# Two transposers for one tile: TensorE takes the lower halves of the probabilities in the first two batches

## The chip, the cores and the metric

The kernel runs on one core of one Trainium2 chip. The metric is the device time of one execution in microseconds (us). Beside it there is a trace of one profiled execution; its own time and its span are in the table further down.

## The reference

An attention layer, then two feed-forward layers, all in fp32: 4 batches, 8 heads, 576 positions, head size 64.

```python
scores = scale * np.matmul(q, k.transpose(0, 1, 3, 2))
h = np.maximum(x @ w1 + b1, 0.0)               # x[i, j]: a function of the positions i and j
scores = scores + (h @ w2).transpose(2, 0, 1)[None]
attn = np.exp(scores - np.max(scores, axis=-1, keepdims=True))
attn = attn / (np.sum(attn, axis=-1, keepdims=True) + 1e-09)
x = np.matmul(attn, v)                         # 2304 tokens x 512
h = x @ w_in;  solu = h * softmax(h)           # 1024 wide
x = (layer_norm(solu) * g_ln) @ w_out
out = (sigmoid(x @ w_gate) * (x @ w_val)) @ w_out2     # 1536 wide
```

The weights of the feed-forward layers come as 8-byte floats. Every fp32 factor of a product is split into a high and a low fp16 part, and three fp16 products (high by high, high by low, low by high) are summed.

## The kernel before, in words

**Attention is cut into 72 ticks** (the list `ticks`, filled by `block`). A tick is 128 queries of two heads against all 576 keys of a batch. A block has 16 ticks for 256 queries of two batches, or 4 ticks ("M") for the last 64 queries of two batches together; batches 0 and 1 are ticks 0 to 35, batches 2 and 3 are ticks 36 to 71. The first element of a tick, `bp`, is 0 or 1 for the two pairs of batches.

**One tick's work** passes through five functions. `a_qk` puts the scores into PSUM (TensorE, L530). `a_soft` adds the bias and takes the maximum (VectorE, L550), scales the maximum (ScalarE, L555) and takes the exponential (ScalarE, L557) into the tile `p` of 2 x 576 fp32. `a_split` makes the fp16 tile `p16` of 2 x 1152 columns: the high part is a cast, on VectorE in every fourth tick (L566) and on ScalarE in the others (L568); the low part is `p` minus the high part on GpSimd, 2 x 512 columns first (L569), then the 2 x 64 columns of the last keys (L570), which fill the second half of a block that the high part's last 64 columns begin. So `p16` has 18 blocks of 128 columns, 9 for each head: 5 with the high part (the fifth is half high, half low) and 4 with the low part of 512 keys. One DMA, issued on SyncE's queue (L572), transposes all 18 into the tile `pt`. `a_pv` multiplies `pt` with V (TensorE, L590; 28 products a tick, 56 of half the width in an M tick) into `xps`. `a_x` and `a_xt` divide by the sums, and transpose the result on TensorE (L636).

**The order.** The loop at the end of the attention emits, in step t: `a_qk(t)`, `a_soft(t)`, `a_split(t-1)`, `a_x(t-5)`, some items of side work, preparation of Q, K and V (`prep_q` L280 to L283, `prep_k` L241 to L244, `prep_v` L254 and L255; their transposes go through PSUM), `a_pv(t-4)`, `a_xt(t-5)`. A planner orders the instructions of every engine from these, by priority and by its own estimate of the times. From the step in which the side work has passed `open_moe` on, TensorE alone is bound to the written order (`manual_schedule`).

**The side work** is first the bias of the later query blocks (masks on VectorE L393, products on TensorE L444, sums on VectorE L460 and L464, stores to memory) and the decoding and splitting of the weights of the first feed-forward layer (loads L660; ScalarE L172, L683, L667 and L668; VectorE L173, L174 and L177; GpSimd L181 and L669). After `open_moe` it is the first feed-forward layer of finished token tiles (TensorE `hps` L732, `ltp` L777, `x2ps` L791), three items a step. `hps` and `x2ps` are sums that are built over several items and hold their PSUM buffer meanwhile.

**Buffers.** `p16` has 2 buffers at first and 3 after `open_moe`, `pt` 3 and then 4. PSUM is cut into `ps_s` (2 buffers of two banks, scores), `ps_v` (1, `xps`) and `ps_m` (3 buffers of one bank), through which go the transposes of Q, K, the attention's result and the feed-forward layer (`qtp`, `ktp`, `xtp`, `ltp`), half of the bias products (`bp`), `hps` and `x2ps`.

After the attention come the weights of the second feed-forward layer and its products (L1149 to L1339); these lines are the same before and after.

Of the kernel before, what the change touches and what calls it, by code (L numbers as in the profile page):

```python
# [9 lines left out]
F16 = mybir.dt.float16  # L10
BF16 = mybir.dt.bfloat16
I32 = mybir.dt.int32
ACTF = mybir.ActivationFunctionType
ALU = mybir.AluOpType
# [78 lines left out]
def attn_moe_kernel(  # L93
# [7 lines left out]
    act, dve, pool, pe, sp = nc.scalar, nc.vector, nc.gpsimd, nc.tensor, nc.sync  # L101
    AX = mybir.AxisListType.X

    def enter(stack, name, bufs=1, side="left", space=None):
        kw = {} if space is None else {"space": space}
        if space is None:
            kw["reuse_waits"] = "tile"
            kw["side"] = side
        return stack.enter_context(tc.tile_pool(name=name, bufs=bufs, **kw))
# [5 lines left out]
    const = enter(ctx, "const")  # L115
# [7 lines left out]
    ps_m = enter(pss, "ps_m", 3, space=PSUM)  # L123
    ps_v = enter(pss, "ps_v", 1, space=PSUM)

    ones_sb = const.tile([128, 128], F32, name="ones_sb")
    id_sb = const.tile([128, 128], F32, name="id_sb")
    sc = const.tile([128, 32], F32, name="sc")
    gs = const.tile([128, 8], F32, name="gs")
    nhalf = const.tile([128, 1], F32, name="nhalf")  # L130
# [33 lines left out]
    def flat(a):  # L164
        return a.rearrange("b h s d -> (b h s d)").rearrange("(p f) -> p f", p=128)
# [27 lines left out]
    def ring(nm, shape, dt, tag=None):  # L193
        r = rings[nm]
        n = turn.get(nm, 0) % len(r)
        turn[nm] = n + 1
        return r[n].tile(shape, dt, name=nm, tag=tag or nm)


    raws, KT, VT, QT = {}, {}, {}, {}  # L200
# [4 lines left out]
    def load_raw(src, b, hp, nm):  # L205
        waiting.append((src, b, hp, nm))
        load_waiting()
# [52 lines left out]
    def load_q(key):  # L260
        bp, qd, hp, b = key
        if qd == "M":
            t = qraw_p.tile([128, 2, 2, D], F32, name="qraw", tag="qraw")
            for par in range(2):
                sp.dma_start(out=t[64 * par:64 * par + 64, 0],
                             in_=q[2 * bp + par, 2 * hp:2 * hp + 2, 512:576, :].rearrange("h p d -> p h d"))
        else:
            t = qraw_p.tile([128, 2, 2, D], F32, name="qraw", tag="qraw")
            for h in range(2):
                sp.dma_start(out=t[:, :, h, :], in_=q[2 * bp + b, 2 * hp + h, 256 * qd:256 * qd + 256, :]  # L270
                             .rearrange("(p r) d -> p r d", r=2))
        raws[key] = t
# [215 lines left out]
    def store0(t, hp):  # L488
        sp.dma_start(out=bias_d[t, :, 2 * hp:2 * hp + 2, :], in_=gb0[t][:, 2 * hp:2 * hp + 2])
# [7 lines left out]
    def load_bias(tk):  # L497
        bp, qd, hp, r, _, bset = tk
        key = (bp, qd, hp, r, bset)
        if key in brt:  # L500
            return
        if (bp, qd) == (0, 0):
            brt[key] = [gb0[r][:, 2 * hp + hh, :] for hh in range(2)]
            return
        n = 8 + 2 * (nbr[0] % 4)
        nbr[0] += 1
        t = gk[0][:, n:n + 2, 0:S]
        if qd == "M":
            for par in range(2):
                sp.dma_start(out=t[64 * par:64 * par + 64], in_=bias_d[4, 0:64, 2 * hp:2 * hp + 2, :])  # L510
        else:
            sp.dma_start(out=t, in_=bias_d[2 * qd + r, :, 2 * hp:2 * hp + 2, :])
        brt[key] = [t[:, hh, :] for hh in range(2)]

    st1, st2, st3, xps, sums, xns = {}, {}, {}, {}, {}, {}
# [44 lines left out]

    def a_split(i):
        pp = st2.pop(i)
        p16 = ring("p16", [128, 2, 1152], F16)
        hi = p16[:, :, 0:576]
        if i % 4 in HI_DVE:
            dve.tensor_copy(hi, pp)  # L566
        else:
            act.activation(out=hi, in_=pp, func=ACTF.Copy)  # L568
        pool.tensor_tensor(out=p16[:, :, 640:1152], in0=pp[:, :, 0:512], in1=hi[:, :, 0:512], op=ALU.subtract)  # L569
        pool.tensor_tensor(out=p16[:, :, 576:640], in0=pp[:, :, 512:576], in1=hi[:, :, 512:576], op=ALU.subtract)  # L570
        pt = ring("pt", [128, 2, 9, 128], F16)
        sp.dma_start_transpose(out=pt.rearrange("p r c q -> p (r c) q"), in_=p16.rearrange("p r c -> p (r c)"))  # L572
        st3[i] = pt

    def pv_seq(vt, hh, lhs):
        seq = []
        for c in range(5):
            seq.append((lhs(c), vt[:, hh, c]))
            seq.append((lhs(c), vt[:, hh, 5 + c]))
        for c in range(4):  # L580
            seq.append((lhs(5 + c), vt[:, hh, c]))
        return seq

    def a_pv(i):
        bp, qd, hp, r, b, bset = ticks[i]
        pt = st3.pop(i)

        def run(seq, o):
            for n, (a, b_) in enumerate(seq):
                pe.matmul(o, a, b_, start=(n == 0), stop=(n == len(seq) - 1))  # L590

        if qd == "M":
            x = ps_v.tile([128, 512], F32, name="xps", tag="v")
            for hh in range(2):
                for par in range(2):
                    po = slice(64 * par, 64 * par + 64)
                    run(pv_seq(VT[2 * bp + par, hp], hh, lambda c: pt[:, hh, c, po]),
                        x[po, 64 * hh:64 * hh + 64])
            xps[bp, qd, hp, bset] = x
        else:  # L600
            key = (bp, qd, hp, bset)
            if key not in xps:
                xps[key] = ps_v.tile([128, 512], F32, name="xps", tag="v")
            x = xps[key]
            for hh in range(2):
                o = 256 * bset.index(b) + 128 * r + 64 * hh
                run(pv_seq(VT[2 * bp + b, hp], hh, lambda c: pt[:, hh, c, :]), x[:, o:o + 64])

    def a_x(i):
        bp, qd, hp, r, b, bset = ticks[i]  # L610
# [193 lines left out]
    ticks, tiles, ready = [], [], []  # L804
# [102 lines left out]
    def stats(src, w):  # L907
        a = nst[0]
        n = src.shape[1] // w
        for i in range(n):  # L910
            t = raw_p.tile([128, w], F32, name="sraw", tag="sraw")
            sp.dma_start(out=t, in_=src[:, w * i:w * i + w])
            j = sj_p.tile([128, w], BF16, name="sj", tag="sj")
            act.activation(out=j, in_=t, func=ACTF.Square, accum_out=stat[:, nst[0]:nst[0] + 1])
            nst[0] += 1
        return (a, nst[0])
# [13 lines left out]
    bs["mid"] = load_mid(bs["sign"])  # L930
    ck = stats(flat(k), SW)
    sp.dma_start(out=id_sb, in_=ident)
    load_q((0, 0, 0, 0))
    load_raw(k, 0, 0, "k")
    with tc.high_priority(1000):
# [70 lines left out]
    def side_step(t):  # L1006
        if nxt[0] is None or (t is not None and nxt[0][0] > t):
            return False
        nxt[0][1]()
        nxt[0] = next(it, None)  # L1010
        return True

    def until(key):
        while key not in done:
            assert side_step(None)
# [3 lines left out]
    for t in range(nticks + LAG_PV + LAG_X + 1):  # L1019
        if not own and "open" in done:  # L1020
            own.append(in_order.enter_context(tc.manual_schedule(engines={mybir.EngineType.PE})))
        with tc.high_priority(PRIO):
            for f in at.get(t, []):
                f()
        for u in range(t, t + 3):
            if u < nticks:
                for tt in {0: (), 1: (2, 3), "M": (4,)}[ticks[u][1]]:
                    until(("bias", tt))
                load_bias(ticks[u])
        with tc.high_priority(PRIO):  # L1030
            if t < nticks:
                a_qk(t)
                a_soft(t)
            if 0 <= t - 1 < nticks:
                a_split(t - 1)
            if 0 <= t - LAG_PV - LAG_X < nticks:
                a_x(t - LAG_PV - LAG_X)
        if t % 2 == ST0 % 2 and 0 <= t - ST0 < 16:
            store0((t - ST0) // 2 % 2, (t - ST0) // 4)
        for n in range(NB if "s" in glob else NB0):  # L1040
            side_step(t)
            if n == 0:
                with tc.high_priority(PRIO):
                    for f in late.get(t, []):
                        f()
        with tc.high_priority(PRIO):
            if 0 <= t - LAG_PV < nticks:
                a_pv(t - LAG_PV)
            if 0 <= t - LAG_PV - LAG_X < nticks:
                a_xt(t - LAG_PV - LAG_X)  # L1050
# [322 lines left out]
    for g in range(2, 5):  # L1373
        n = sizes[g]
# [75 lines left out]
```

## Time and profile before

| what | us |
|---|---|
| three runs | 1086.48, 1092.41, 1091.01 |
| their median | 1091.01 |
| the profiled execution's own time | 1090.94 |
| its span, first to last instruction | 1089.2 |
| busy in the span: TensorE, VectorE, ScalarE, GpSimd | 914.1, 777.0, 619.7, 404.3 |
| mean granted TensorE clock | 0.893 of full speed |
| bytes moved by DMA | 146.58 MB |

In the rows below "A <- B" reads "A waited for B"; SPq is SyncE's queue, which only issues DMAs, and its durations are the time that an issue took. The DMA share of a stretch is the busy share of 16 DMA engines; packets are counted where they start, so it can pass 1.

### The profile page before, as it was taken

The page shows a single profiled execution, that of the slowest core. Times are in us where ns is not written, and L with a number is a line of the kernel's source. Part 1 is how long each engine was busy: PE and PEld are TensorE (multiplying, and loading weights), DVE is VectorE, ACT ScalarE, POOL GpSimd, SP SyncE. Part 2 cuts the span into 40 slices and gives each one's busy share as a digit, 9 for nine tenths or more (in the row PEclk, how much of TensorE's full clock was granted, in tenths as well). Part 3 has the DMA queues.
Part 4 walks back from the last instruction along what each step waited for, and adds up shares of the span by engine and source line. Part 5 has one row for each costly group of instructions (what it writes and reads, how often), then busy time and mean ns, then how long its engine had stood idle before and what let it go on. Part 6 is the DMA issues. An engine that isn't in the chain of part 4 may idle for free.

```text
span 1089.2 us, 24462 instructions
## 1 busy us (share of the span) xinstructions
PE 914.1 (84%) x9806; PEld 655.5 (60%) x9806; DVE 777.0 (71%) x1605; ACT 619.7 (57%) x1283; POOL 404.3 (37%) x370
## 2 busy tenths in 40 slices
PE   3645674669688879989999788897999999999998
PEld 3634554546466658667776466444477866865873
DVE  6875998895666676666765999989973871881760
ACT  4786776765676788877883676753442331331331
POOL 2356355653555565545561365749000000000000
PEclk9655566778898999989999898999999999999999
DMA  7999999489879899998975535511001010001001
GB/s 226 289 293 254 215 218 244 99 182 230 165 162 191 197 194 180 195 189 196 189 113 169 163 111 174 187 56 39 30 11 58 1 49 30 1 1 39 2 1 39
DMA packets 261442, 146.58 MB, mean 135 GB/s; under 512 B 217680, under 2 KB 231504, under 8 KB 261328
## 3 DMA queue, kind: packets, MB, share of 16 engines
q1 hardware_dynamic: 259264, 143.18, 55.2%
q0 software_dynamic: 1536, 1.58, 0.6%
q8 instruction: 77, 1.26, 0.5%
q14 instruction: 37, 0.30, 0.1%
q10 hardware_dynamic: 528, 0.26, 0.1%
HBM read 82.46 MB, written 20.05 MB: 94 GB/s over the span
## 4 chain that ended last, share of the span: by engine, by line
PE 30%; DVE 13%; DMA 4%; ACT 2%; issue 2%; SPq 0%; ACTq 0%; DVEq 0%
PE prod L1262 15%; PE ops L1330 10%; DVE fs L1186 4%; DVE w2f L177 2%; DVE w2f L174 2%; DMA wraw<-in_moe_w_val_dram 2%; PE x2ps L791 2%; PE s_ps L1300 1%; DVE w2s L1186 1%; DMA wraw<-in_moe_w_gate_dram 1%; DVE gv L1168 1%; PE hps L732 1%; DMA wraw<-in_moe_w_out_dram 1%; DVE fr L1306 1%; PE xps L590 1%
## 5 line engine op out<-in xcount | busy, mean ns | idle before, releaser
L569 POOL TENSOR_TENSOR p<-p,p 128x1024 f16<-128x1024 f32 x72 | 155.7, 2162 | 155.0 <-ACT p L568 116.6
L1186 DVE TENSOR_TENSOR fr<-prod,fr 128x512 f32<-128x512 f32 x126 | 85.1, 687 | 94.0 <-PE prod L1262 92.3
L1330 PE MATMUL ops<-w2f,gv 128*128 128x512 f16 x648 | 143.4, 379 | 2.7 <-POOL w2f L669 1.5
L557 ACT ACTIVATE p<-p,m,sc 128x576 f32<-128x576 f32 x144 | 123.9, 861 | 2.8
L791 PE MATMUL x2ps<-lt,w1f 128*128 128x128 f16 x1728 | 111.9, 226 | 12.4 <-DVE lt L780 11.7
L550 DVE CUSTOM_DVE_ANT_0 p<-s_ps,gk 128x576 f32<-128x576 f32 x144 | 104.2, 751 | 20.3 <-PE s_ps L530 16.4
L791 PEld LDWEIGHTS <-w1f 128*128 128x128 f16 x1728 | 105.7, 102 | 21.1 <-issue 17.0
L1300 PE MATMUL s_ps<-xb,w2f 128*128 128x512 f16 (+1 forms) x576 | 101.5, 333 | 15.0 <-DVE fr L1306 10.7
L590 PE MATMUL xps<-gk,pt 128*128 128x64 f16 (+1 forms) x2240 | 89.2, 204 | 23.0 <-DMA pt<-p 23.0
L1330 PEld LDWEIGHTS <-gv 128*128 128x128 f16 x648 | 63.4, 98 | 74.4 <-issue 1.5
L590 PEld LDWEIGHTS <-pt 128*128 128x128 f16 (+1 forms) x2240 | 83.3, 108 | 34.8 <-DMA pt<-p 25.5
L530 PE MATMUL s_ps<-gk,qt 64*128 64x288 f16 (+1 forms) x960 | 92.1, 321 | 13.2 <-DVE m L550 6.9
L444 PEld LDWEIGHTS <-mask 128*128 128x128 f16 (+1 forms) x1312 | 64.5, 122 | 51.1 <-issue 18.0
L1300 PEld LDWEIGHTS <-w2f 128*128 128x128 f16 x576 | 57.3, 100 | 58.7 <-issue 22.7
L1262 PEld LDWEIGHTS <-w2f 128*128 128x128 f16 x864 | 84.5, 98 | 11.8 <-issue 1.1
L1167 ACT ACTIVATE gv<-fr 128x512 f16<-128x512 f32 (+1 forms) x60 | 34.9, 585 | 83.7 <-DVE fr L1320 70.5
L732 PE MATMUL hps<-w1f,xt 128*128 128x512 f16 x312 | 76.7, 396 | 0.6 <-DVE qt L283 0.6
L555 ACT ACTIVATE m<-m,sc 128x1 f32<-128x1 f32 x144 | 40.6, 286 | 54.1 <-DVE m L550 53.9
L444 PE MATMUL bp<-rhs,mask 128*128 128x64 f16 (+1 forms) x960 | 51.3, 224 | 22.5 <-DVE gb L464 13.9
L530 PEld LDWEIGHTS <-qt 64*128 64x128 f16 (+1 forms) x960 | 47.3, 106 | 36.8 <-issue 16.8
L1262 PEld LDWEIGHTS <-w2s 128*128 128x128 f16 x648 | 63.4, 98 | 7.3
L732 PEld LDWEIGHTS <-xt 128*128 128x128 f16 x384 | 37.1, 102 | 49.8 <-issue 15.5
(194 smaller groups left out, 1795.2 us busy)
## 6 DMA issues: line engine op xcount, KB each, us to landing
gk<-bias_d SPq DMA_DIRECT2D x24, 576.0 KB
wraw<-in_moe_w_out_dram SPq DMA_DIRECT2D x20, 512.0 KB
wraw<-in_moe_w_gate_dram SPq DMA_DIRECT2D x12, 512.0 KB
wraw<-in_moe_w_val_dram SPq DMA_DIRECT2D x12, 512.0 KB
sraw<-in_q_dram SPq DMA_DIRECT2D x12, 384.0 KB
sraw<-in_k_dram SPq DMA_DIRECT2D x12, 384.0 KB
sraw<-in_v_dram SPq DMA_DIRECT2D x12, 384.0 KB
bias_d<-gk SPq DMA_DIRECT2D x8, 576.0 KB
```

The lines of the kernel that those rows point to most:

```text
L444: pe.matmul(big[0:np_, jj // 8, o:o + 64], lhsT, rhs[i].rearrange("p c h g -> p (c h g)"), start=(i == 0), stop=(i == 1),)
L530: pe.matmul(ss[hh][p0:p1, n, 0:288], qt[rows, nr * ql + r, p0:p1], kt[rows, o:o + 288], start=(m == 0), stop=(m == 2))
L550: dve.tensor_tensor_reduce(out=pp[:, hh].rearrange("p (i j) -> p i j", i=2), in0=ss[hh][:, :, 0:288], in1=bi.rearrange("p (i j) -> p i j", ...
L557: act.activation(out=pp[:, hh], in_=pp[:, hh], func=ACTF.Exp, bias=m[:, 2 + hh:3 + hh], scale=col(C), accum_out=sm[:, c + hh:c + hh + 1])
L569: pool.tensor_tensor(out=p16[:, :, 640:1152], in0=pp[:, :, 0:512], in1=hi[:, :, 0:512], op=ALU.subtract)
L590: pe.matmul(o, a, b_, start=(n == 0), stop=(n == len(seq) - 1))
L732: pe.matmul(h, xt[:, xl, kk, off:off + 128], win16[:, 2 * kk + n, wl], start=(kk == 0 and xl == 0 and wl == 0), stop=(kk == 3 and xl == 1),)
L791: pe.matmul(ps[:, dc], wout16[:, f, wl, 128 * dc:128 * dc + 128], lt[:, ll, f], start=(n == 0), stop=(n == 23))
L1186: dve.tensor_tensor(out=out_, in0=a, in1=b, op=op)
L1262: pe.matmul(p[:, jf, 0:nn], w(wl, kk, jf), x(xl, kk), start=(m == 0), stop=(m == 5))
L1300: pe.matmul(ps[:, 0:n], w[:, 4 * (j // 4) + c, wl, o:o + 128], xx[:, 0:n, c, xl, :], start=(m == 0), stop=(m == 11))
L1330: pe.matmul(ps, gvs[j // 4][:, gl, j % 4, 128 * tt:128 * tt + 128], w2h16[2][:, j, wl], start=(m == 0), stop=(m == 35))
```

## The change

The columns of `p16` are put in another order: first the five blocks of the high part of either head (10 blocks, with the low part of the last 64 keys in them), then the four low blocks of either head. GpSimd makes the low part of the last 64 keys first and that of the 512 keys second. For ticks of the first two batches the DMA transposes the first 10 blocks only. The other 8 are transposed by TensorE with an fp16 identity into one `ps_m` buffer, and ScalarE copies that buffer into the same `pt` (`a_lo`, emitted one step after `a_split` of the same tick, before `a_x`). `a_pv` takes its blocks by their new numbers. For ticks 36 to 71 one DMA transposes all 18 blocks as before.

```diff
+    id16 = const.tile([128, 128], F16, name="id16")
...
-        p16 = ring("p16", [128, 2, 1152], F16)
-        hi = p16[:, :, 0:576]
+        p16 = ring("p16", [128, 2304], F16)
+        hi = p16[:, 0:1280].rearrange("p (r c) -> p r c", r=2)
+        lo = p16[:, 1280:2304].rearrange("p (r c) -> p r c", r=2)
         if i % 4 in HI_DVE:
-            dve.tensor_copy(hi, pp)
+            dve.tensor_copy(hi[:, :, 0:576], pp)
         else:
-            act.activation(out=hi, in_=pp, func=ACTF.Copy)
-        pool.tensor_tensor(out=p16[:, :, 640:1152], in0=pp[:, :, 0:512], in1=hi[:, :, 0:512], op=ALU.subtract)
-        pool.tensor_tensor(out=p16[:, :, 576:640], in0=pp[:, :, 512:576], in1=hi[:, :, 512:576], op=ALU.subtract)
-        pt = ring("pt", [128, 2, 9, 128], F16)
-        sp.dma_start_transpose(out=pt.rearrange("p r c q -> p (r c) q"), in_=p16.rearrange("p r c -> p (r c)"))
+            act.activation(out=hi[:, :, 0:576], in_=pp, func=ACTF.Copy)
+        pool.tensor_tensor(out=hi[:, :, 576:640], in0=pp[:, :, 512:576], in1=hi[:, :, 512:576], op=ALU.subtract)
+        pool.tensor_tensor(out=lo, in0=pp[:, :, 0:512], in1=hi[:, :, 0:512], op=ALU.subtract)
+        pt = ring("pt", [128, 18, 128], F16)
+        n = 10 if on_pe(i) else 18
+        sp.dma_start_transpose(out=pt[:, 0:n], in_=p16[:, 0:128 * n])
         st3[i] = pt
+        if on_pe(i):
+            los[i] = lo
+
+    def on_pe(i):
+        return ticks[i][0] == 0
+
+    def a_lo(i):
+        if i not in los:
+            return
+        lo, pt = los.pop(i), st3[i]
+        ps = ps_m.tile([128, 2, 4, 128], F16, name="plo", tag="m")
+        for hh in range(2):
+            for c in range(4):
+                pe.transpose(ps[:, hh, c], lo[:, hh, 128 * c:128 * c + 128], id16)
+        act.activation(out=pt[:, 10:18], in_=ps.rearrange("p h c q -> p (h c) q"), func=ACTF.Copy)
...
     sp.dma_start(out=id_sb, in_=ident)
+    pool.tensor_copy(id16, id_sb)
...
                 a_split(t - 1)
+            a_lo(t - 2)
```

## Rows read from the trace of the kernel before

**Rows 1.** Page, part 2: busy share in tenths, 40 slices of the span.
```profile
DMA  7999999489879899998975535511001010001001
```

**Rows 2.** Windows: busy us of PE, PEld, DVE, ACT, POOL; granted clock, DMA share, GB/s.
```profile
82.00:255.00 173.00, 112.80 (x1525) 84.87 (x1523) 143.99 (x290) 116.43 (x252) 94.21 (x80) 0.63 0.90 204
115.00:185.00 70.00, 49.15 (x584) 35.92 (x581) 67.16 (x124) 48.94 (x105) 39.60 (x35) 0.62 1.00 229
255.00:395.00 140.00, 116.50 (x1583) 83.90 (x1580) 94.47 (x234) 100.91 (x225) 76.73 (x72) 0.93 0.86 183
395.00:587.00 192.00, 179.71 (x2721) 137.77 (x2720) 120.86 (x343) 146.99 (x325) 101.13 (x84) 0.96 0.92 178
```

**Rows 3.** Windows of L569 alone (one a tick): GpSimd busy us and count.
```profile
82.00:255.00 173.00, 42.01 (x19) 0.63 0.90 204
255.00:395.00 140.00, 43.27 (x20) 0.93 0.86 183
395.00:587.00 192.00, 70.38 (x33) 0.96 0.92 178
```

**Rows 4.** VectorE's waits, 82 to 255 us: total us, times, longest.
```profile
DVE w1f L173 <- ACT w1f L172: 6.0, 7, 1.8
DVE p L550 <- PE s_ps L530: 5.0, 4, 2.2
DVE gk L255 <- ACT gk L254: 3.5, 2, 3.2
...
DVE xn L623 <- PE xps L590: 2.8, 1, 2.8
```

**Rows 5.** Waits of TensorE and of SyncE's queue, 82 to 255 us.
```profile
PE xps L590 <- DMA pt<-p: 23.0, 10, 6.7
PE bp L444 <- DVE gb L464: 13.9, 9, 5.0
SPq L572 <- POOL p L570: 20.0, 6, 5.2
```

**Rows 6.** Timeline, 181 to 189 us: start us, us, what [idle before].
```profile
181.01 5.54 SPq L572 DMA_TRANSPOSE pt<-p  x1
...
188.75 1.68 PE L590 MATMUL xps<-gk,pt 128*128 128x64 f16 x28 [6.68 <-DMA pt<-p]
```

**Rows 7.** Windows around two lone transposes late in the attention; columns as rows 2.
```profile
559.00:563.00 4.00, 4.00 (x79) 3.61 (x76) 3.80 (x11) 3.63 (x8) 1.53 (x1) 1.00 0.81 152
566.00:570.00 4.00, 4.00 (x66) 3.06 (x64) 1.09 (x6) 3.93 (x10) 3.36 (x4) 1.00 0.88 166
```

**Rows 8.** Tile pt: issue of the transposing DMA, ns least/median/most.
```profile
L572 SPq DMA_TRANSPOSE pt<-p x72: 2401/3434/6899, 88.6 to 573.5; - x72
```

**Rows 9.** Groups by shape: busy us, mean ns of one | idle before.
```profile
L569 POOL TENSOR_TENSOR p<-p,p 128x1024 f16<-128x1024 f32 x72 | 155.7, 2162 | 155.0 <-ACT p L568 116.6 <-issue 26.7 <-DVE x L797 4.3
...
L777 PE MATMUL ltp<-id_sb,e 128*128 128x128 f32 x144 | 21.9, 289 | 8.4 <-DVE mm L743 4.7 <-DVE gk L244 2.8 <-DVE qt L283 0.7
...
L779 ACT ACTIVATE lt<-ltp 128x512 f16<-128x512 f32 x36 | 20.3, 585 | 2.5 <-PE ltp L777 2.4
...
L653 ACT ACTIVATE xt<-xtp 128x256 f16<-128x256 f32 x32 | 12.0, 375 | 8.1 <-DVE xt L654 4.8 <-PE xtp L636 3.2
```

**Rows 10.** TensorE's timeline, two runs of one kind of product: start us, us.
```profile
294.59 3.74 PE L791 MATMUL x2ps<-lt,w1f 128*128 128x128 f16 x35 [2.17 <-DVE lt L780]
...
322.80 4.19 PE L791 MATMUL x2ps<-lt,w1f 128*128 128x128 f16 x72
```

**Rows 11.** TensorE's waits, 255 to 395 us, first and fourth of twelve kinds.
```profile
PE ktp L241 <- DVE mm L743: 3.8, 2, 2.0
...
PE ktp L241 <- DVE qt L283: 3.1, 1, 3.1
```

**Rows 12.** Timeline: a tick's low part, and the scores two ticks later.
```profile
328.83 2.14 POOL L569 TENSOR_TENSOR p<-p,p 128x1024 f16<-128x1024 f32 x1 [0.76 <-POOL e L768]
...
333.67 0.91 PE L530 MATMUL s_ps<-gk,qt 64*128 64x288 f16 x12
```

More of the change, by code (lines that the diff above doesn't have):

```diff
@@ L562, in a_split @@
         pp = st2.pop(i)
-        p16 = ring("p16", [128, 2, 1152], F16)
-        hi = p16[:, :, 0:576]
+        p16 = ring("p16", [128, 2304], F16)
+        hi = p16[:, 0:1280].rearrange("p (r c) -> p r c", r=2)
+        lo = p16[:, 1280:2304].rearrange("p (r c) -> p r c", r=2)
         if i % 4 in HI_DVE:
-            dve.tensor_copy(hi, pp)
+            dve.tensor_copy(hi[:, :, 0:576], pp)
         else:
-            act.activation(out=hi, in_=pp, func=ACTF.Copy)
-        pool.tensor_tensor(out=p16[:, :, 640:1152], in0=pp[:, :, 0:512], in1=hi[:, :, 0:512], op=ALU.subtract)
-        pool.tensor_tensor(out=p16[:, :, 576:640], in0=pp[:, :, 512:576], in1=hi[:, :, 512:576], op=ALU.subtract)
-        pt = ring("pt", [128, 2, 9, 128], F16)
-        sp.dma_start_transpose(out=pt.rearrange("p r c q -> p (r c) q"), in_=p16.rearrange("p r c -> p (r c)"))
-        st3[i] = pt
+            act.activation(out=hi[:, :, 0:576], in_=pp, func=ACTF.Copy)
[4 more added lines that the diff above has]
+        sp.dma_start_transpose(out=pt[:, 0:n], in_=p16[:, 0:128 * n])
+        st3[i] = pt
+        if on_pe(i):
+            los[i] = lo
+    los = {}
+    def on_pe(i):
[9 more added lines that the diff above has]
+        act.activation(out=pt[:, 10:18], in_=ps.rearrange("p h c q -> p (h c) q"), func=ACTF.Copy)
     def pv_seq(vt, hh, lhs):
@@ L577, in pv_seq @@
         for c in range(5):
-            seq.append((lhs(c), vt[:, hh, c]))
-            seq.append((lhs(c), vt[:, hh, 5 + c]))
+            seq.append((lhs(5 * hh + c), vt[:, hh, c]))
+            seq.append((lhs(5 * hh + c), vt[:, hh, 5 + c]))
         for c in range(4):
-            seq.append((lhs(5 + c), vt[:, hh, c]))
+            seq.append((lhs(10 + 4 * hh + c), vt[:, hh, c]))
         return seq
@@ L596, in a_pv @@
                     po = slice(64 * par, 64 * par + 64)
-                    run(pv_seq(VT[2 * bp + par, hp], hh, lambda c: pt[:, hh, c, po]),
+                    run(pv_seq(VT[2 * bp + par, hp], hh, lambda c: pt[:, c, po]),
                         x[po, 64 * hh:64 * hh + 64])
@@ L606, in a_pv @@
                 o = 256 * bset.index(b) + 128 * r + 64 * hh
-                run(pv_seq(VT[2 * bp + b, hp], hh, lambda c: pt[:, hh, c, :]), x[:, o:o + 64])
+                run(pv_seq(VT[2 * bp + b, hp], hh, lambda c: pt[:, c, :]), x[:, o:o + 64])
     def a_x(i):
```

## The prediction

> **What bounds the kernel now.** I read the slices of the page first, then windows by stage, then who waited for whom in each. The slices [rows 1] show the DMA engines at nine tenths through most of the first half, which is the attention. The windows [rows 2] and the count of ticks [rows 3] cut the attention into three stages with different limits. *Stage 1*, 82 to 255 us, has 19 ticks (9.1 us each): bias and weight decoding run beside them. VectorE is busy 143.99 of 173 us, and 67.16 of the 70 in its middle; the DMA share is 0.90. *Stage 2*, 255 to 395 us, has 20 ticks (7.0 us each): TensorE is busy 116.50 of 140 us and bound to the written order, ScalarE 100.91, VectorE 94.47; the DMA share is 0.86, but no wait of TensorE for `pt` is among its kinds [rows 11]: its idle 23.5 us are waits for results that come back through ScalarE and VectorE, mostly to free a `ps_m` buffer. *Stage 3* has 33 ticks of 5.8 us with TensorE at 179.71 of 192. What follows the attention has other work and other limits.
>
> So in stage 1 the bound is VectorE with holes in it, in stage 2 it is TensorE with holes in it. The holes of stage 1 come to 173 - 144 = 29 us. Four kinds of them [rows 4] go back to a DMA: VectorE waits for decoded weights (6.0) and for V (3.5), whose loads share the DMA engines, and for scores (5.0) and finished sums (2.8) that stand on TensorE behind a product with `pt`. TensorE itself waited 23.0 us there for `pt`, ten times [rows 5]. One instance [rows 6]: an issue at 181.01, landed and used at 188.75 only.
>
> **The change, part by part.**
>
> *The DMA.* Two lone transposes took 4 x 0.81 = 3.24 and 4 x 0.88 = 3.52 us of all 16 DMA engines [rows 7], say 3.4 us for 18 blocks. Ten blocks are 1.9 us if the time goes by blocks, so 1.5 us less; the ends are 0 (if it does not) and 1.6. In stage 1 the 19 transposes are 65 us of 173 x 0.90 = 156 us of DMA work, and 29 us of that goes, 18%. The issue on SyncE's queue took 3.43 us in the median [rows 8]; by blocks it is 1.5 us shorter too, but issue and transfer overlap, so I count 1.5 us a transpose once. Of VectorE's holes, those behind `pt` (5.0 + 2.8 = 7.8) belong to ten waits of 2.3 us; 1.5 us off each is 65%, 5.1 us. Those behind loads (9.5) shrink by the 18%, 1.7 us. Sum: -7. The other ends: 0, since VectorE is 96% busy in the middle of the stage, and -18, all four kinds (17.3) gone.
>
> The Trainium skill ("Advanced Engine Details and Errata", X-Bar Transpose) calls transposing DMAs as fast as plain ones and expects 350 to 400 GB/s. The trace has 4 us x 152 GB/s = 608 KB in 3.24 us, 188 GB/s, so here the page is off by two. By the page the eight blocks (262 KB) would save about 0.7 us a transpose, an estimate, and stage 1 would gain 3 to 4 us less than I count.
>
> *GpSimd's order.* The small subtraction now comes first, so the DMA no longer waits behind the 2.16 us of L569 [rows 9]. SyncE's queue waited for GpSimd six times for 20.0 us in stage 1 [rows 5], so up to 6 x 2.1 us come earlier. This is the same wait as above, seen one step sooner; it is why I take the 65% and not less. If the DMA went on waiting for the whole tile, this is 0.
>
> *TensorE.* Eight fp16 transposes a tick, 36 ticks. No fp16 transpose is in the trace. The nearest row is a product of the same shape, 128x128 fp16: 4.19/72 = 58 ns at the full clock, 3.74/35 = 107 ns where the clock was at the lower level [rows 10]. The other end is an fp32 transpose's mean, 289 ns [rows 9]. I take 58 and 107: 0.46 us a tick in stage 2, 0.86 us in stage 1. In stage 1 TensorE is idle 60 us of 173 and the 17 sets (15 us) lie beside VectorE's work. In stage 2 there are 19 sets (`a_lo` comes two steps after the scores): 19 x 0.46 = 8.8 us, at the granted 0.93 about 9.5; TensorE is busy 83% of the stage, and that share falls on the path: +7.9.
>
> *ScalarE.* One copy of 128x1024 from PSUM a tick. From 585 ns for 512 and 375 for 256 columns [rows 9] the slope is 0.82 ns, so 585 + 420 = 1.0 us; the upper end is twice 585, 1.17. Its load goes in stage 1 from 67% to 77%, in stage 2 from 72% to (100.9 + 19)/140 = 86%. In its queue behind the copy stand the exponentials and the evictions of `qtp`, `ktp` and V, for which TensorE and VectorE wait. In stage 2 I count +1.5 us: the one long wait for `qt` and two like it [rows 11], each later by half a copy. In stage 1 +1.
>
> *A `ps_m` buffer.* `plo` takes one of three from its first transpose to the end of the copy. In stage 1 that is 0.9 + 1.0 us and perhaps 1 us of queue, 3 of 9.1 us: a ninth of the three. TensorE already waited 13.9 us there for VectorE to free bias buffers [rows 5]; a ninth more is +1.5, of which VectorE, being the bound, feels about 1. In stage 2 it is in the waits counted above; the end on the other side is the slow rival.
>
> *The new wait.* TensorE's transposes stand in written order right behind the scores of two ticks later. An instance [rows 12]: the low part starts at 328.83 and with the small subtraction ends at 331.4; the scores two ticks on end at 333.67 + 0.91 = 334.6. 3.2 us to spare, so it costs nothing; without that cover all of TensorE's side items and the next scores queue behind it.
>
> *The rest.* The fp16 identity is one small GpSimd copy at the start: 0. Ticks 36 to 71 do the same work in the same amounts: 0, and what the first half wins or loses is carried through stage 3 and behind it one to one.
>
> *The sum.* Stage 1: -7 + 1 + 1 = -5. Stage 2: +7.9 + 1.5 = +9.4. Together +4.4, against the profiled execution's own 1090.94 (span 1089.2, and 1.7 around it): 1095. The median of the runs is 1091.01, the same within 0.1. Differences under 0.5%, 5.5 us, a measurement of this kernel can't tell from none. The forecast's own range is -4 to +12, 1087 to 1103.
>
> **The rivals.**
>
> *The DMA was the real bound of stage 1 (faster).* With two `p16` buffers, a cast waits for the transpose of two ticks before, so each transpose lies on a loop. For it: the share of 1.00 for 70 us [rows 2], 23 us of waits for `pt`. Against it: VectorE's 67 of 70 us in the same stretch. Then all 17.3 us of holes go, and TensorE's extra work in stage 2 falls into its 23.5 idle us more than its share, half of +9.4: -17.3 + 4.7 = -13, 1078.
>
> *The third `ps_m` buffer is missing in stage 2 (slower).* Price: one more wait in each of the 19 steps, of the length that stage 2 has now, 23.5 us over the some 20 times of [rows 11], 1.2 us, half of them in front of work that waits anyway: +11. It decides once TensorE, in a step that prepares K, asks for its next buffer before the copy has left ScalarE's queue. For it: the waits are already there. Against it: in steps with `x2ps` alone nothing asks for 4 us [rows 10]. 1095 + 11 = 1106.
>
> *Each transpose is paid at its full time.* At 289 ns [rows 9] a set is 2.3 us, 19 sets 44 us, 83% of it 36 instead of 7.9: 1124. The fp32 transposes have that mean although they come in fours, but waits and the lower clock are in it. The Trainium skill ("TensorE: Matmul & The Clock Gate", Part 4) speaks against the change in this way: about 275 ns for a transpose in a kernel; no run here shows one in fp16.
>
> *Nothing is felt,* both ends hidden: 1091, within 4.
>
> **How the numbers follow.** Forecast 0.42, faster rival 0.33, `ps_m` 0.15, full-price transposes 0.04, nothing 0.06. Slower by over 0.5%: 38% of the forecast's range, and the two slow rivals: 0.16 + 0.15 + 0.04 = 0.35. Faster: 85% of its rival and a trace of the forecast: 0.29. Within: 0.36. The range 1075 to 1107 leaves out the far ends of the fast rival, half of the `ps_m` one and the 1124, some 0.18.
>
> **What would show it.** Right: transposing DMAs of about 1.9 us, TensorE's waits for `pt` in stage 1 at half or less, VectorE's busy share of stage 1 up from 83%, the first scores of stage 2 some 5 us sooner, and stage 2 longer by about 9. A set of eight transposes at 0.5 us, a copy at 1.0. Wrong: stage 1 shorter by over 12 us, or stage 2 not longer, or waits of TensorE on `plo` or for its copy that come to over 10 us.

## The result and the profile after

The changed kernel takes 1094.4 us in the median of 17 runs (1091.17 to 1098.35), the kernel before 1090.0 in the median of as many. The ratio is 1.0055, 95% interval 1.0039 to 1.0071: slower by 6.0 us (4.3 to 7.7). The ratio is formed from fast runs alone, which leaves out one run of the kernel before with 1156.6 us; the medians of all runs differ by 4.4 us. The profiled execution took 1091.17 us and is the shortest of its 17, so its trace shows where waits stand better than it shows the difference.

Page of the changed kernel, parts 1 and 2:

```profile
PE 920.9 (85%) x10094; PEld 660.1 (61%) x10094; DVE 770.3 (71%) x1605; ACT 650.7 (60%) x1319; POOL 405.3 (37%) x371
...
DMA  8999894748466579999965536511001010001001
```

TensorE has 7 us more than before, ScalarE 31, and the DMA digits of the first two batches, the fourth to the fifteenth, fell from mostly 8 and 9 to mostly 4 to 8 [rows 1]. Stages 1 and 2, columns as in [rows 2]:

```profile
82.00:255.00 173.00, 118.50 (x1611) 89.60 (x1609) 138.14 (x285) 127.25 (x260) 96.05 (x78) 0.67 0.74 174
255.00:395.00 140.00, 117.35 (x1670) 86.82 (x1669) 90.06 (x224) 111.44 (x230) 69.79 (x70) 0.95 0.62 140
```

The DMA share of stage 1 fell from 0.90 to 0.74, and yet VectorE, which the prediction takes for the bound there, does less in the same 173 us: 138.14 against 143.99. TensorE's waits in stage 1 (total, times, longest), the changed kernel:

```profile
PE tot L149 <- DVE acc L147: 8.3, 1, 8.3
PE xps L610 <- DVE xn L643: 6.1, 2, 5.3
PE xps L610 <- DMA pt<-p: 5.5, 3, 2.2
...
PE plo L592 <- DVE gb L465: 4.7, 5, 1.7
PE qtp L281 <- ACT pt L593: 4.6, 2, 4.3
...
PE plo L592 <- DVE qt L284: 3.3, 1, 3.3
PE bp L445 <- ACT pt L593: 3.3, 4, 1.4
PE xps L610 <- ACT pt L593: 2.3, 1, 2.3
```

The wait for `pt` fell from 23.0 to 5.5 us [rows 5]. In its place stand waits of the new work: for a free `ps_m` buffer before the transposes (`plo` <- `gb`, `qt`: 8.0) and for ScalarE's copy (L593: 10.2), 18.2 together. They replace in part the wait of the bias products for the same buffers, 13.9 before and 2.7 now. TensorE's own work in the stage grew by 5.7 us, and its waits for `xn` and `tot`, which VectorE brings late, by 6.1 and 5.5. VectorE's waits of the same stretch:

```profile
DVE p L551 <- PE s_ps L531: 8.9, 7, 3.1
DVE acc L147 <- ACT wjunk L703: 5.4, 1, 5.4
DVE qt L284 <- ACT qt L283: 5.3, 3, 2.9
```

It now waits more for scores that TensorE brings late (5.0 before, [rows 4]) and for ScalarE. Its other three kinds of holes of [rows 4] shrank: decoded weights from 6.0 to 4.9 us, V from 3.5 to 1.0, finished sums from 2.8 to 0.9.

The prices. Tile `plo` of the changed kernel (ns min/median/max), and a set, the eight transposes of one tick, in TensorE's timeline (start us, us):

```profile
L592 PE MATMUL plo<-id,p x288: 216/219/314, 96.2 to 388.0; 128*128 128x128 f16 x144
L593 ACT ACTIVATE pt<-plo x36: 997/1018/1027, 99.3 to 389.0; 128x1024 f16<-128x1024 f16 x36
```
```profile
277.23 0.62 PE L592 MATMUL plo<-id,p 128*128 128x128 f16 x8
277.68 1.46 PE L752 MATMUL hps<-w1f,xt 128*128 128x512 f16 x6
```

From 277.23 to the next product at 277.68 a set takes 0.45 us, forecast 0.46. Where the granted clock was 0.50, the lower level, the eight span 1.04 us with the end of the last one (at 172.98, shown under e7), against 0.62 so measured here; the forecast was 0.86 from start to start. The copy takes 1.02 us, forecast 1.0. One transposing DMA ran alone (windows: DMA share and GB/s last; then GpSimd and SyncE's queue, changed kernel):

```profile
176.50:178.00 1.50, 1.50 (x28) 1.38 (x26) 1.03 (x3) 1.50 (x3) 0.51 (x2) 0.50 0.00 0
177.90:180.70 2.80, 0.14 (x3) 0.00 (x0) 2.57 (x1) 0.70 (x2) 2.80 (x3) 0.50 0.60 113
```
```profile
177.49 0.43 POOL L571 TENSOR_TENSOR p<-p,p 128x128 f16<-128x128 f32 x1 [5.36 <-ACT p L570]
177.88 2.12 POOL L572 TENSOR_TENSOR p<-p,p 128x1024 f16<-128x1024 f32 x1
177.95 1.36 SPq L575 DMA_TRANSPOSE pt<-p  x1
```

With the DMA engines idle ahead of it, 2.80 x 0.60 = 1.68 us of all 16 for ten blocks, against 3.24 and 3.52 for 18 [rows 7]; this issue takes 1.36 us, the median before was 3.43 [rows 8], and it starts while the big subtraction runs. So every price was as forecast; what they cost the kernel was not.

### The profile page after: what moved, and what is told of

Same layout as the page of the kernel before. It is cut to its first block, busy times and chain, and to the rows that moved or that the text cites. A ratio compares the mean times of both kernels' runs of the same rounds, so it can differ in the third digit from the quotient of the medians.

```text
span 1089.4 us, 25069 instructions
## 1 busy us (share of the span) xinstructions
PE 920.9 (85%) x10094; PEld 660.1 (61%) x10094; DVE 770.3 (71%) x1605; ACT 650.7 (60%) x1319; POOL 405.3 (37%) x371
## 4 chain that ended last, share of the span: by engine, by line
PE 34%; DVE 14%; DMA 2%; issue 2%; ACT 2%; POOL 0%; SPq 0%; DVEq 0%; ACTq 0%
PE prod L1284 15%; PE ops L1352 10%; DVE fs L1208 4%; PE x2ps L811 3%; DVE w2f L175 2%; PE hps L752 2%; DVE w2f L178 2%; PE s_ps L1322 1%; DVE w2s L1208 1%; PE xps L610 1%; DVE gv L1190 1%; DMA wraw<-in_moe_w_val_dram 1%; DVE w2f L174 1%; PE s_ps L531 1%; DVE fr L1328 1%
## 5 line engine op out<-in xcount | busy, mean ns | idle before, releaser
L572 POOL TENSOR_TENSOR p<-p,p 128x1024 f16<-128x1024 f32 x72 | 158.1, 2196 | 0.0
L811 PE MATMUL x2ps<-lt,w1f 128*128 128x128 f16 x1728 | 105.6, 221 | 11.2 <-DVE lt L800 11.1
L811 PEld LDWEIGHTS <-w1f 128*128 128x128 f16 x1728 | 100.3, 99 | 19.5 <-issue 16.0
L610 PE MATMUL xps<-gk,pt 128*128 128x64 f16 (+1 forms) x2240 | 89.5, 202 | 13.9 <-DVE xn L643 6.1
L571 POOL TENSOR_TENSOR p<-p,p 128x128 f16<-128x128 f32 x72 | 32.0, 445 | 168.9 <-ACT p L570 118.8
L1284 PEld LDWEIGHTS <-w2f 128*128 128x128 f16 x864 | 84.5, 98 | 11.8 <-issue 1.1
L445 PEld LDWEIGHTS <-mask 128*128 128x128 f16 (+1 forms) x1312 | 60.4, 116 | 48.5 <-issue 25.5
L1284 PEld LDWEIGHTS <-w2s 128*128 128x128 f16 x648 | 63.4, 98 | 7.3
L445 PE MATMUL bp<-rhs,mask 128*128 128x64 f16 (+1 forms) x960 | 51.8, 219 | 17.3 <-DVE gk L465 7.7
```

The costliest lines, as they stand in the source:

```text
L445: pe.matmul(big[0:np_, jj // 8, o:o + 64], lhsT, rhs[i].rearrange("p c h g -> p (c h g)"), start=(i == 0), stop=(i == 1),)
L572: pool.tensor_tensor(out=lo, in0=pp[:, :, 0:512], in1=hi[:, :, 0:512], op=ALU.subtract)
L811: pe.matmul(ps[:, dc], wout16[:, f, wl, 128 * dc:128 * dc + 128], lt[:, ll, f], start=(n == 0), stop=(n == 23))
L1284: pe.matmul(p[:, jf, 0:nn], w(wl, kk, jf), x(xl, kk), start=(m == 0), stop=(m == 5))
```

## The experiments

All were timed in five rounds; the ratios are to runs of the kernel before on the same chip, and a thousandth is 1.09 us. The expectations count a low part by its tick; a tick's set stands in TensorE's order two steps after its scores. The landmarks below are start times (us) of TensorE's groups in the traces, one profiled execution each.

| run | tick 15's product with `pt` | first `hps` | tick 20's product | tick 35's | first of the second layer (L1284) | ratio |
|---|---|---|---|---|---|---|
| before | 253.0 | 258.2 | 289.2 | 388.6 | 826.9 | 1 |
| change | 255.4 | 264.1 | 294.2 | 396.0 | 827.1 | 1.0055 |
| e1_layout | 250.2 | 255.0 | 285.3 | 387.2 | 821.9 | 0.9986 |
| e2_early | 253.9 | 259.2 | 284.4 | 386.0 | 817.8 | 0.9984 |
| e3_late | 251.7 | 259.1 | 292.4 | 395.2 | 832.6 | 1.0082 |
| e4_dma_alone | 244.8 | 249.6 | 275.4 | 376.4 | 809.8 | 0.9876 |
| e5_cost_alone | 255.2 | 264.3 | 295.6 | 401.0 | 831.0 | 1.0095 |
| e7_no_copy | 251.9 | 259.2 | 287.5 | 389.9 | 823.4 | 0.9999 |
| e11_first11 | 250.2 | 255.0 | 285.4 | 384.9 | 819.3 | 0.9961 |
| e12_24to35 | 249.2 | 254.0 | 283.8 | 391.3 | 825.8 | 1.0009 |
| e13_19to23 | 250.4 | 258.1 | 292.8 | 393.6 | 834.1 | 1.0057 |
| e14_two_parts | 250.9 | 256.2 | 281.4 | 383.4 | 819.1 | 0.9954 |
| e8_dve | 251.7 | 259.1 | 286.0 | 392.8 | 827.6 | 1.0052 |
| e10_later | 256.8 | 262.8 | 293.5 | 395.3 | 825.7 | 1.0064 |

How finely this can be read: from tick 35 to L1284 all kernels do the same work, and the table has 430 to 441 us for it. Up to tick 15, e1, e3, e12 and e13 do the same work, and they reach its product at 249.2 to 251.7. So a difference of up to 3 us at tick 15 in a single trace is not a finding, and behind tick 35 one of 10 us is none; one that repeats over runs is.

**e1_layout: the columns, GpSimd's order and the identity, without the new work.**

```diff
     def on_pe(i):
-        return ticks[i][0] == 0
+        return False
```

> The changed kernel with no tick on TensorE: all 18 blocks by the DMA everywhere, so that only the new column order, GpSimd's order (small subtraction first) and the fp16 identity are left of the change. Theory A (the 4 to 6 us are the work of the transposes and copies): the time of the kernel before, 1090, within 3 us, or up to 3 us less since the issue of the DMA no longer stands behind the big subtraction if that mattered. Theory B (the planner laid the instructions out in another order, and that alone costs): 1094 to 1096 already here.

Measured 0.9986 (0.9968 to 1.0004), 1086.3 us. The other order of columns and subtractions and the planner's other choices with it are not the cost; this is the baseline for what the rest costs.

**e2_early and e3_late: one part of the ticks each.**

```diff
-        return ticks[i][0] == 0
+        return i < 19                # e2_early
+        return 19 <= i < 36          # e3_late
```

> TensorE transposes for ticks 0 to 18 only (stage 1); ticks 19 to 35 by the DMA. Theory A (the sum of the prediction): 5 us faster than before, 1085, since the relief of the DMA is worth 7 and the copies and the buffer cost 2. Theory C (the trace of the changed kernel: the weights' sum of squares is ready 7 us sooner, at 186 instead of 193, but the first product of the feed-forward layer starts 6 us later): ScalarE's copies and the ps_m buffer take the gain back inside stage 1, so 0 to +4 us, 1090 to 1094.

> TensorE transposes for ticks 19 to 35 only (stage 2). Theory A: +9 us over before, 1099: 0.46 us of TensorE a tick, and 1.5 us by ScalarE. Theory C: half of that or less, +3 to +5, because stage 1 has carried the rest. In the trace the sets should be 0.46 us apart from what follows and the wait for pt on TensorE in stage 1 as before (23 us).

Measured 0.9984 (0.9964 to 1.0005), -1.7 us, and 1.0082 (1.0053 to 1.0110), +8.9 us. The late ticks cost what the prediction counted for stage 2 (+9.4). The early ones win less than its -5; they add up to +7.2, about the whole.

**e4_dma_alone and e5_cost_alone: the relief without the work, and the work without the relief.** e4 leaves out the low part of 512 keys in ticks 0 to 35: the products read high blocks in its place. e5 transposes all 18 blocks by DMA and throws the copies away.

```diff
-        if on_pe(i):
-            los[i] = lo
...
-   lambda c: pt[:, c, :]
+   lambda c: pt[:, c if c < 10 or not on_pe(i) else c - 10, :]      # e4
```
```diff
-        n = 10 if on_pe(i) else 18
+        n = 18
...
-        act.activation(out=pt[:, 10:18], ...)
+        spare = ring("spare", [128, 8, 128], F16)
+        act.activation(out=spare, ...)                                # e5
```

> In ticks 0 to 35 the DMA transposes 10 blocks and nothing transposes the other 8: the products that would read the low blocks read high blocks instead, the same count and shape. So the low part of the probabilities is left out; GpSimd still makes it. This is the relief of the DMA alone. Theory A: 7 us faster than before, 1083, all in stage 1, nothing in stage 2. Theory C: 7 to 12 us faster, since the cost that took it back is gone. Rival (VectorE alone bounds stage 1): within 3 us of before.

> The cost alone: in ticks 0 to 35 the DMA transposes all 18 blocks, and TensorE transposes the low blocks as well and ScalarE copies them, into a spare tile that nothing reads. If relief and cost add up (the change is +6, the relief alone -13.5): +19, 1107. Theory A (the sum of the prediction, +2 in stage 1 and +9 in stage 2): +11, 1099. If most of the cost lies beside waits for the DMA while these last: +5 or less.

Measured 0.9876 (0.9847 to 0.9905), -13.5 us, and 1.0095 (1.0071 to 1.0119), +10.4. The relief is worth twice the -7 of the prediction; the cost beside the long DMA is its +11.4 within the interval. But -13.5 + 10.4 = -3, and the change is at +6: 9 us are neither. The window of stage 1 and the waits for `pt` show part of the reason; e1, then e4, then e5's wait:

```profile
82.00:255.00 173.00, 110.74 (x1588) 83.75 (x1584) 148.96 (x296) 117.59 (x256) 90.87 (x80) 0.66 0.91 203
```
```profile
PE xps L610 <- DMA pt<-p: 20.1, 8, 4.3
```
```profile
82.00:255.00 173.00, 116.59 (x1662) 85.81 (x1659) 148.92 (x305) 122.89 (x269) 100.72 (x83) 0.68 0.81 184
```
```profile
PE xps L608 <- DMA pt<-p: 26.3, 12, 5.0
```
```profile
PE xps L611 <- DMA pt<-p: 13.0, 10, 2.6
```

With the short DMA alone TensorE waits *longer* for `pt` (26.3 us; 23.0 before, 20.1 in e1), and yet tick 15 is reached 5.4 us before e1. VectorE's busy share does not tell the two apart: 148.92 of 173 us in e4, 148.96 in e1. With the long DMA and the new work TensorE waits 13.0. So the 5.5 of the change are no sign of relief: TensorE is late itself, and the transfer has time to land. The new work costs 5.0 us up to tick 15 beside the long DMA (255.2 - 250.2), where part of it lies in waits for `pt` (13.0 are left of e1's 20.1), and 10.6 beside the short one (255.4 - 244.8).

**e7_no_copy: short DMA and transposes, no copy.** As in e4 the products read high blocks; the low part of 512 keys is left out in ticks 0 to 35.

```diff
-        act.activation(out=pt[:, 10:18], in_=ps.rearrange("p h c q -> p (h c) q"), func=ACTF.Copy)
```

> The change without ScalarE's copies: TensorE transposes the low blocks into the ps_m buffer, nothing reads it, and the products that would read the low blocks read high blocks instead (the low part of the probabilities is left out). If ScalarE's 36 us are the cost: near the relief alone, -10 to -13 against before, 1075 to 1078. If TensorE's 288 transposes are the cost: near the change, 0 to +6, 1088 to 1094. Theory A (in stage 2, 7.9 of the 9.4 us are TensorE's): -5 to 0.

Measured 0.9999 (0.9980 to 1.0018). Beside e4 the transposes with their buffer cost 13.4 us, of them 7.1 up to tick 15; the copy, with the buffer that it holds, another 6.1. In the change a product with `pt` also has to wait for the copy, in e5 and e7 none does: that wait is within these 6.1 us and was not timed by itself. The transposes alone, without it, cost about as much beside the short DMA (13.4) as transposes and copies beside the long one (10.4). An instance in the changed kernel (timeline, stage 1):

```profile
172.98 1.04 PE L592 MATMUL plo<-id,p 128*128 128x128 f16 x8
...
174.68 0.72 ACT L687 ACTIVATE wtmp<-w1f,sc 128x512 f32<-128x512 f32 x1
...
175.31 1.00 ACT L593 ACTIVATE pt<-plo 128x1024 f16<-128x1024 f16 x1
...
176.37 1.67 PE L610 MATMUL xps<-gk,pt 128*128 128x64 f16 x28 [2.35 <-ACT pt L593]
```

The set ends at 174.02, the copy starts at 175.31 behind weight decoding on ScalarE, and TensorE waits 2.35 us for it.

**e8_dve: the copies on VectorE.**

```diff
-        act.activation(out=pt[:, 10:18], in_=ps..., func=ACTF.Copy)
+        dve.tensor_copy(pt[:, 10:18], ps...)
```

> The change with the copies on VectorE instead of ScalarE. VectorE takes 0.68 us for 512 columns from PSUM (ltp), so some 1.2 us a copy, 17 of them, 20 us, in stage 1, where it is 83% busy and the bound; 23 us in stage 2, where it is 67% busy. If VectorE bounds stage 1: 10 to 20 us slower than the change, 1104 to 1114. If the length of ScalarE's queue is what a copy costs: as the change or up to 5 us faster.

Measured 1.0052 (1.0034 to 1.0070), as the change. The copies on VectorE, and its window of stage 1:

```profile
L593 DVE COPY pt<-plo x36: 675/681/692, 102.0 to 387.0; 128x1024 f16<-128x1024 f16 x36
```
```profile
82.00:255.00 173.00, 117.43 (x1710) 89.95 (x1711) 153.90 (x313) 118.87 (x255) 96.86 (x80) 0.71 0.77 181
```

A copy takes 0.68 us, not the 1.2 of the expectation (ScalarE: 1.02), so 17 of them are 12 us. VectorE works 153.90 of the 173 us, 15.8 more than in the change, and tick 15 comes no later (251.7 against 255.4). So VectorE had room in stage 1 of the changed kernel and did not bound it by itself. Which engine copies makes no difference that can be measured in the kernel's time; the lead of 8 us that this trace has at tick 20 is 3 at tick 35 and gone at L1284.

**e12_24to35 and e13_19to23: the late ticks in two parts.**

```diff
-        return ticks[i][0] == 0
+        return 24 <= i < 36          # e12_24to35
+        return 19 <= i < 24          # e13_19to23
```

> TensorE transposes for ticks 24 to 35 only, the steady part of stage 2. Theory A (83% of TensorE's time, 0.46 us a tick, falls on the path wherever it stands): 12 x 0.46 x 0.83 = 4.6 and 1 by ScalarE, +5 against before, 1092 to 1093. Theory D (from tick 20 on the traces of the change and of the runs without late copies are equally long, 101 to 103 us to tick 35, so the loss sits where the feed-forward work begins): +2 or less.

> TensorE transposes for ticks 19 to 23 only, where the feed-forward work begins. Theory A: 5 x 0.46 x 0.83 = 1.9 and 0.4, +2 against before. Theory D: most of the 9 us that ticks 19 to 35 cost, +5 to +7, 1093 to 1094.

Measured 1.0009 (0.9988 to 1.0029), +1.0 us, and 1.0057 (1.0037 to 1.0078), +6.2. Five ticks, in which the feed-forward work begins and TensorE enters its written order, cost more than the twelve behind them. What they cost can be read off by laying the changed kernel beside e2, which is the same up to tick 18. TensorE's timeline, the changed kernel:

```profile
259.92 0.91 PE L531 MATMUL s_ps<-gk,qt 64*128 64x288 f16 x12
263.66 0.62 PE L592 MATMUL plo<-id,p 128*128 128x128 f16 x8 [2.83 <-POOL p L572]
264.12 5.74 PE L752 MATMUL hps<-w1f,xt 128*128 128x512 f16 x18
...
283.01 0.27 PE L242 MATMUL ktp<-id_sb,kv 64*128 64x64 f32 x1 [2.35 <-DVE mm L779]
283.21 2.76 PE L752 MATMUL hps<-w1f,xt 128*128 128x512 f16 x12
...
293.76 0.66 PE L797 MATMUL ltp<-id_sb,e 128*128 128x128 f32 x4 [1.73 <-DVE gk L245]
294.25 0.98 PE L610 MATMUL xps<-gk,pt 128*128 128x64 f16 x28
```

and e2_early:

```profile
258.39 0.91 PE L531 MATMUL s_ps<-gk,qt 64*128 64x288 f16 x12
259.24 4.06 PE L752 MATMUL hps<-w1f,xt 128*128 128x512 f16 x18
...
274.58 0.27 PE L242 MATMUL ktp<-id_sb,kv 64*128 64x64 f32 x1 [1.55 <-DVE mm L779]
...
283.95 0.66 PE L797 MATMUL ltp<-id_sb,e 128*128 128x128 f32 x4 [0.81 <-DVE gk L245]
284.45 0.98 PE L610 MATMUL xps<-gk,pt 128*128 128x64 f16 x28
```

From these scores to tick 20's product it is 34.33 us against 26.06, +8.3: the wait for GpSimd's low part and the first set +3.35 (4.20 against 0.85), the 18 products behind the wait +1.68 (5.74 against 4.06, at the clocks shown further down), three more sets +1.4, and +1.7 in K's and `ltp`'s waits. The last of these is ScalarE's queue; changed kernel:

```profile
289.25 1.02 ACT L593 ACTIVATE pt<-plo 128x1024 f16<-128x1024 f16 x1 [1.12 <-PE plo L592]
...
292.25 0.87 ACT L244 ACTIVATE gk<-ktp,sc 128x512 f16<-128x512 f32 x2
```

K's eviction stands behind the copy and two exponentials. The same entry, from scores to the first `hps`, has a wait for GpSimd in the other runs with tick 19's set there too: 2.37 us in e5, 1.97 in e3 and e13, 1.48 in e7, 1.35 in e8.

**e10_later: from tick 17 on the set is emitted one step later.**

```diff
-            a_lo(t - 2)
+            a_lo(t - 2 if t - 2 < 17 else t - 3)
```

> The change with the transposes of ticks 17 to 35 one step later in TensorE's written order. In the trace of the change TensorE waits 2.83 us for GpSimd's low part right before the first product of the feed-forward layer, and 8 of the 9 us lost against the relief alone stand between the products with V of ticks 15 and 20. If that wait and the late start are the cost: 3 to 6 us faster than the change, 1088 to 1091. If it is the work itself: as the change, within 2 us.

Measured 1.0064 (1.0041 to 1.0086), as the change. TensorE's timeline in e10:

```profile
261.53 0.91 PE L531 MATMUL s_ps<-gk,qt 64*128 64x288 f16 x12
262.37 0.62 PE L592 MATMUL plo<-id,p 128*128 128x128 f16 x8
262.83 4.05 PE L752 MATMUL hps<-w1f,xt 128*128 128x512 f16 x18
...
280.60 0.27 PE L242 MATMUL ktp<-id_sb,kv 64*128 64x64 f32 x1 [2.35 <-DVE mm L779]
280.80 4.41 PE L752 MATMUL hps<-w1f,xt 128*128 128x512 f16 x12
```

The wait is gone and the 18 products run in 4.05 us again, but this trace reaches tick 15 1.4 us later (256.8), and twelve products at 280.80 now take 4.41 us at a granted clock of 0.62, where the change has 2.76 at 1.00. That is not e10's doing: they take 4.13 in the kernel before and 4.45 in e1 as well. What the trace wins at the entry does not arrive at the end: the wait is a part of these ticks' length, and not shown to be what makes the kernel slower.

**e11_first11 and e14_two_parts: the change in fewer ticks.**

```diff
-        return ticks[i][0] == 0
+        return i < 11                      # e11_first11
+        return i < 11 or 15 <= i < 19      # e14_two_parts
```

> TensorE transposes for ticks 0 to 10 only. In the traces of the change, of ticks 0 to 18 alone and of the relief alone the weights' sum of squares is ready at 186 to 188 us instead of 193, and from there to tick 15 only the runs with copies lose it again (the relief alone does not). If the copies after tick 10 are what loses it: 5 us faster than before, 1083. If the 6 us go whatever comes after (the bias work on VectorE bounds the rest of the stage): within 2 us of before.

> TensorE transposes for ticks 0 to 10 and 15 to 18. Ticks 0 to 10 alone were 4 us faster than before; in the traces with ticks 15 to 18 relieved too (0 to 18, and the relief alone) the stretch from tick 15's product with V to tick 20's is 30.5 us instead of 35 to 36. If that stretch keeps its gain: 8 us faster than before, 1079. If the gain there is only what ticks 11 to 14 had lost before: as ticks 0 to 10 alone, -4.

Measured 0.9961 (0.9944 to 0.9978), 1083.38 us, and 0.9954 (0.9934 to 0.9973), 1082.8 us: both beat the kernel before, by 4.2 and 5.0 us, and the change by about 1%. The step from 11 to 15 ticks can't be told from none. The table has the four ticks in e14 all the same: from the first `hps` to tick 20 it takes 25.2 us, as e2 (25.2) and e4 (25.8), which also have short DMAs in ticks 15 to 18 and no sets behind them; before, e1, e11 and e12, with long DMAs there, take 29.8 to 31.0. In e14 2.5 of these 5 us are lost again by tick 35 (102.0 against 99.5 us in e11).

## Why the prediction was right in sum and wrong in its parts

The sum (+4.4 forecast, +6.0 measured) and the sign hold, but that the sum does is luck: the relief is -13.5 us instead of -7, and the work that e4 leaves out costs 19.5 (6.0 + 13.5) instead of the +11.4 forecast. Two misses of 6.5 and 8 us nearly cancel. The parts:

- **The relief, -7 in stage 1.** Right for stage 1, too small for the kernel. By the landmarks the short DMA alone (e4) reaches tick 15 5.4 us before e1 and 8.2 before the kernel before. The step that failed is that it ends there: another 4.5 us come between the first `hps` and tick 20 (25.8 against 30.3), and e2 and e14 repeat it (25.2). The prediction gave stage 2 no relief, because TensorE waits for no `pt` there. By the waits the DMA reaches it through VectorE. VectorE's waits, 250 to 290 us, of e1 and then of e4:

```profile
DVE hs L763 <- DMA bias_d<-gb: 4.2, 1, 4.2
...
DVE p L551 <- DMA gk<-bias_d: 2.0, 1, 2.0
```
```profile
DVE p L551 <- DMA gk<-bias_d: 1.3, 1, 1.3
```

  The stores and loads of the bias hold VectorE 6.2 us there beside long transposes, 1.3 beside short ones. In the other traces with long ones in ticks 15 to 18 these waits come to 2.3 (before) to 10.0 (e13), in those with short ones to 0; e5, later at tick 15, has long ones and none. Not all of the 4.5 us is theirs: twelve `hps` products take 2.76 us in e4 at a granted clock of 1.00 and 4.45 in e1 at 0.60.
- **TensorE in stage 1, 0.** This is the step that failed most: "the 17 sets (15 us) lie beside VectorE's work". They cost 7.1 us up to tick 15 (e7 against e4). TensorE's 60 idle us were not free for them. By which wait they cost it stays open: in the change VectorE waits 8.9 us for scores instead of 5.0, and the sets 8.0 for buffers; but in e7, without the copies, VectorE waits 4.3 for scores (82 to 255 us), and instead ScalarE's cast into `p16` waits 4.6 for sets of earlier ticks. The premise under the zero, that VectorE bounds stage 1, does not hold in the changed kernel: 12 us of copies moved onto VectorE (e8) cost nothing that shows.
- **ScalarE and `ps_m` in stage 1, +1 and +1.** Mis-sized if anything: 3.5 us by tick 15 (255.4 - 251.9), little more than traces of equal work differ there, and 6.1 us for the copies of both stages. The prediction's own alarm, waits of TensorE on `plo` or for its copy of over 10 us, went off in stage 1 with 4.7 + 3.3 + 4.6 + 3.3 + 2.3 = 18.2, against which the bias products wait 11.2 less. Together this item and the one above cost 10.6 up to tick 15 and not 2, the relief is used up, and the early ticks come out at -1.7 instead of -5.
- **Stage 2, +9.4.** The size is right (e3, +8.9), the division by ticks is not: 0.41 us a tick for 19 ticks would be 5 for e12 and 2 to 3 for e13, which measured +1.0 and +6.2. Against e1, which has the same layout, e12 is +2.5; its own trace shows 5.6 us more than e1's from tick 20 to 35, the changed kernel's none (101.8 against 101.9). What a set costs in the steady part is thus between 0 and the forecast and stays open.
- **The new wait, 0.** The cover of 3.2 us [rows 12] was read in the steady part. At the entry it is missing once, for 2.83 us and a lower clock behind it. e10 takes the wait away and is no faster, so 0 is within what it is worth, for another reason.
- **Behind tick 35, one to one.** Not shown: the profiled execution has 7.4 us to make up at tick 35 and 0.2 at L1284. With a spread of 430 to 441 us for that stretch it can't be told what is carried.
- **What would show it.** The prices and the halved waits for `pt` came, and said nothing of the gain. VectorE's busy share of stage 1 was to rise from 83% and fell to 80%; it is no safe sign either, being 86% in e1 and e4 alike and 89% in e8. The first scores of stage 2 were to come 5 us sooner and stage 2 to last 9 longer: by the landmarks tick 15 comes 2.4 us later, and from there to tick 35 it is 140.6 us against 135.6. These two signs failed, and they were the ones to read.

Of the rivals, "the DMA is the real bound" had the size of the relief (-17.3; e4 -13.5) but took TensorE's work as half hidden. The missing `ps_m` buffer is there, in stage 1 (the 8.0 us above) and not where it was looked for: from 255 to 400 us TensorE's waits for the copy come to 1.2 us. Full-price transposes fell with the 0.45 us a set: the Trainium skill ("TensorE: Matmul & The Clock Gate", Part 4) gives about 275 ns for a transpose in a kernel; a single one has 219 ns here, but eight in a row take 0.45 us, 56 ns each: they overlap.

Not settled: by which waits the sets cost 7 us in stage 1, and why the costs of ticks 19 to 23 add up to the end when e10's shorter entry and e14's shorter stretch arrive there only in part. The planner orders other engines anew in each variant, and a kernel with a fixed order was not tried.

## What to carry to other kernels

When work moves from the DMA to the engines, time the relief alone and the cost alone: here -13.5 and +10.4 made +6, since beside the long DMA part of the engines' new work is hidden in the very waits that the relief takes away. A wait that shrinks need not be a gain: TensorE's wait for `pt` fell when TensorE got later, and was longest in the fastest kernel. Read from landmarks of equal work where the time went. And try moving it in a part of the ticks: the first 11 of 36, which hold the stretch with a DMA share of 1.00 [rows 2], gave 0.4%, all 36 lost 0.55%. That the DMA share is what decides was not tested.

## What the runs showed of the hardware that was not expected

A wait of some two microseconds can be paid twice on TensorE, and need not be. Windows over the 18 `hps` products (granted clock third from the right), the changed kernel behind its 2.83 us of waiting, and e2 without it:

```profile
264.10:269.70 5.60, 5.60 (x22) 2.08 (x19) 1.88 (x4) 3.46 (x8) 3.67 (x4) 0.70 1.06 208
```
```profile
259.20:263.20 4.00, 4.00 (x20) 1.64 (x18) 2.60 (x8) 4.00 (x12) 2.67 (x3) 1.00 0.96 305
```

At a mean granted clock of 0.70 (full speed is 2.4 GHz, the lower level 1.2) the same products took 5.74 us instead of 4.06. But a wait of that length does not decide it. Behind 1.97 us of the same wait they took 5.22 us at 0.77 in e13 and 4.05 at 1.00 in e3. Behind 2.35 us of waiting for `mm` the twelve products took 2.76 us at 1.00 in the change and 4.41 at 0.62 in e10. What makes the difference stays open.

A copy of 128x1024 fp16 out of PSUM took 0.68 us on VectorE (e8) and 1.02 on ScalarE.

The transposing DMA of ten blocks moved 2.80 us x 113 GB/s = 316 KB in its 1.68 us, 188 GB/s, the rate of the one with 18 blocks in the prediction: from 18 to 10 blocks its time went by blocks.
